# A shorter lead of the max pass, unit 0's maxima in another order, and rows of maxima sent sooner, in an attention and MLP kernel on one core

## The chip, the cores and the metric

The kernel runs on one core of a Trainium2 chip. The metric is the device time of one execution in microseconds, as the median of three runs. Everything told of the inside of an execution comes from one profiled execution.

## The reference

One layer with adaptive layernorm: 2048 tokens of width 512, 32 query heads of width 16 that share one key head and one value head (MQA), then an MLP of width 1376 with a tanh GELU.

```python
mod = (_silu(c) @ w_mod).reshape(c.shape[0], 6, 1, -1)      # sa, ca, ga, sb, cb, gb
h = _layernorm(x) * (1 + ca) + sa
q = (h @ wq) in 32 heads;  k = h @ wk;  v = h @ wv
p = softmax(q @ k.T * Dh ** -0.5);  o = p @ v
x = x + ga * (o @ wo)
h = _layernorm(x) * (1 + cb) + sb
x = x + gb * (gelu(h @ w1 + b1) @ w2 + b2)
```

All of it is float32. The kernel splits the operands of the large products into a high part and the rest (the names that end in H and L) and adds three products.

## The kernel before

**Units.** The 2048 queries are cut into 8 blocks of 256 (`blocks`), and the 32 heads into 8 groups of four. A pair (block, group) is a unit; there are 64, and eight in a row make a block. For a unit, `sexp` forms the scores, one tile e of 128 keys by 512 for each half of the TensorE array, and ScalarE turns it into p with `exp`; `pv` multiplies p with the values into acc. A unit has 8 key steps K, taken in pairs (X, Y), so four pairs, and each pair has two halves.

**Max pass.** Softmax needs each query's maximum first. `Max.step` forms scores once more with queries as rows (tile m, L505), and VectorE reduces each tile to one column of mx (L510). A unit has 32 such products. When its last column is there, `put_max` reduces mx to mm (L558), turns it (`turned`, L559), and `gather` copies four pieces into mt on POOL (L553), splits mt into mh and ml, and `send` writes mh and ml for both halves into two rows of the unit's query tile qst (four transfers, L548). With these rows in qst, the e product subtracts the maximum by itself. So a unit's first e waits for those transfers.

**Lead.** The max pass runs ahead of the units. `lead[u]` is the number of max products done before unit u starts: those of units 0 to u and 4 * LEAD more. Inside a unit each pair issues 8. `first` and `size` count products.

**Clock of steps.** The order on every engine is the order of the program (`manual_schedule`); nothing is reordered. `clock` counts four steps to a pair, 16 to a unit, and `later(n, fn)` issues fn n steps on, through `due()`, in the order of entry. `put_max` enters its reduce so that it falls on the first step of the next pair, the gather MAX_WAIT[0] = 1 step behind it and the sends MAX_WAIT[1] steps behind it. The steps fix only the order in each queue: SP, which issues nearly all transfers, goes ahead until a transfer has to wait.

**Work beside the units.** Jobs in `queue` hand out batches of products, one batch to a pair at most: the late query projections, and for each finished block `rest` (L719): fetch and normalize the attention output (`norm`), the product with wo (wops), layernorm, two transposes (tp) and modulation, w1 with GELU, w2. In `rest_steps`, when the second wops tile is complete (`add_x`, L827), the statistics st follow one and three steps later, `rstd` (mv on VectorE, then ve and rs on POOL) four steps later and `xhat` (xh on POOL) five steps later; the transposes that read xh are offered eight steps later. For every block but the last this happens in the third unit of the next block: wops is complete in the second pair, and the transposes come in the first pair of the fourth unit. In the units behind that each pair carries one w1 tile; its GELU is finished on POOL (L954, L955, L964, L965 and the split into gH and gL).

**Prologue.** Layernorm, keys, values and the first query projections are laid out by hand in SLOTS: each entry says how many max products to issue and then which steps of other work: "q 1" the second query projection, "v 3" values, "rows" the products of the late modulation rows (modl, L290), "wq" casts of wq on ScalarE (wqH, L335). There `later` does its work at once (`draining`). FIRST_MAX says in which order the products of units 0 and 1 come. `keep_warm` issues products whose result is not used (idle, L285); WARM[3] of them stand just ahead of unit 0.

Of the kernel before, what the change touches and what calls it, by code (L numbers as in the profile page):

```python
# [11 lines left out]
ALU = mybir.AluOpType  # L12
AX = mybir.AxisListType

P = 128
# [3 lines left out]

GELU_R = 0.044715 ** 0.5  # L20

LEAD = 6
LEAD_0 = 6
FIRST_MAX = ((0, 0), (1, 0), (0, 1), (1, 1), (0, 2), (0, 3), (1, 2), (1, 3))
SLOTS = ((2, "keys 1", "keys 1"), (2, "keys 1", "keys 1"), (2, "low 1", "heads 2"), (2, "heads 2", "k 1"), (1, "warm"), (1, "heads 2"), (2, "heads 2", "v 0"),
# [4 lines left out]
MAX_WAIT = (1, 4)  # L30
QBUFS = 4
PREP = 4
BUSY = 5
# [3 lines left out]
TAIL = (4, 8)  # L37
GROUP = 4
NORM_WAIT = 6
WARM = (4, 16, 2, 5)  # L40
MOD_WAIT = 3
AHEAD = 4.5
STIR = ((0, 4, 8, 12), (16, 32, 48, 0))
# [2 lines left out]
def raw(ap):  # L46
    return ap.bitcast(F32)
# [3 lines left out]
def adaln_mqa_mlp(  # L51
# [15 lines left out]
    nc = tc.nc  # L67
    _, S, D = x.shape
# [9 lines left out]
    NKC = S // 512  # L78
# [14 lines left out]
    def pad(pool, nbytes, name):  # L93

        nc.gpsimd.memset(pool.tile([P, nbytes // 4], F32, name=name), 0.0)
# [32 lines left out]
    def split(dst_h, dst_l, src, eng_h, eng_l, between=None):  # L128
        if eng_h is nc.gpsimd:
            eng_h.tensor_scalar(out=dst_h, in0=src, scalar1=1.0, scalar2=0.0, op0=ALU.mult, op1=ALU.add)  # L130
        elif eng_h is nc.scalar:
            eng_h.copy(dst_h, src)
        else:
            eng_h.tensor_copy(out=dst_h, in_=src)
        if between:
            between()
        eng_l.tensor_tensor(out=dst_l, in0=src, in1=raw(dst_h), op=ALU.subtract)  # L137
# [7 lines left out]
    def later(n, fn):  # L145
        if draining[0]:
            fn()
        else:
            pending.append((clock[0] + n, fn))
# [7 lines left out]
    def mm3(ps, pairs, every=0, cost=0, begin=True, end=True):  # L157

        n, last = 0, 3 * len(pairs) - 1
        for wh, wl, xh, xl in pairs:  # L160
            for a, b_ in ((wh, xh), (wl, xh), (wh, xl)):
                nc.tensor.matmul(ps, a, b_, start=begin and n == 0, stop=end and n == last)  # L162
                n += 1
                if every and n % every == 0:
                    yield cost
# [113 lines left out]
    def keep_warm(n, **place):  # L279

        for k in range(n):
            if k == 0 or not place:
                ps = psum.tile([P, BQ], F32, name=f"idle{len(idles)}", **(place or dict(tag="m", bufs=3)))
                idles.append(ps)
            nc.tensor.matmul(ps, wkH[:, 0, :], wkH.rearrange("p k n -> p (k n)"), start=True, stop=True)  # L285
# [84 lines left out]
    def turn1(b, d):  # L370
        ps = psum.tile([P, BQ], F32, name=f"tp{b}_{d}", **ebank())
        for t in range(QT):
            nc.tensor.transpose(ps[:, t * P:(t + 1) * P], xts[b][:, t, d * P:(d + 1) * P], ident)
        tps[b, d] = ps
# [40 lines left out]
    def send_q(b, g, qH, qL):  # L415
        for t, src in enumerate((qH, qL)):
            nc.sync.dma_start(out=dq[b][g][t].rearrange("a r j n -> (a r j) n"), in_=raw(src))
        state["q"] -= 1
        sent.add((b, g))
# [3 lines left out]
    def qpairs(b, g):  # L423
        hH, hL = hts[b]
        gs = slice(g * P, (g + 1) * P)
        return [(wqH[:, k, gs], wqL[:, k, gs], hH[:, k, :], hL[:, k, :]) for k in range(KD)]

    def qtiles(b, g):
        qH = att.tile([P, BQ], F32R, name=f"qH{b}_{g}", tag="xH", bufs=2)
        qL = att.tile([P, BQ], F32R, name=f"qL{b}_{g}", tag="xL", bufs=2)  # L430
        return qH, qL

    def qproj(b, g):

        ps = psum.tile([P, BQ], F32, name=f"qps{b}_{g}", tag="v" if g else "x")
        yield from mm3(ps, qpairs(b, g), 3, 1)
        qH, qL = qtiles(b, g)
        if g == 0:
            nc.scalar.copy(qH, ps)
            nc.vector.tensor_tensor(out=qL, in0=ps, in1=raw(qH), op=ALU.subtract)  # L440
        else:
            q32 = pro.tile([P, BQ], F32, name=f"q32_{b}_{g}", tag="h32", bufs=4)
            nc.scalar.copy(q32, ps)
            split(qH, qL, q32, act, pool)
        send_q(b, g, qH, qL)
        yield -2

# [32 lines left out]
    class Max:  # L480


        def __init__(self):
            def products(u, kcs):
                return [(u, j, t, kc) for kc in kcs for j in range(2) for t in range(blocks[units[u][0]][1] // P)]

            def in_rows(u):
                return [(u, j, t, kc) for j in range(2) for t in range(blocks[units[u][0]][1] // P) for kc in range(NKC)]


            begin = [o for u, kc in FIRST_MAX for o in products(u, [kc])]
            self.todo = [begin + [o for u in range(2, NU) for o in in_rows(u)] for _ in range(2)]
            self.mx, self.left, self.done = {}, list(size), 0

# [34 lines left out]
    def put_max(u, mx):  # L529

        T = blocks[units[u][0]][1] // P
        qst = qsts[u]
        mm = mms[u % 2]
        turned = att.tile([P, 32], F32, name=f"turned{u}", tag="turned", bufs=2)
        if u == 0:
            pad(att, 256, "pad7")
        mt = att.tile([4 * T, P], F32, name=f"mt{u}", tag="mt", bufs=2)
        mh = att.tile([4 * T, P], F32R, name=f"mh{u}", tag="mh", bufs=2)  # L540
        ml = att.tile([4 * T, P], F32R, name=f"ml{u}", tag="ml", bufs=2)

        def send():
            for s in range(2):
                for r, src in ((48, mh), (49, ml)):
                    dst = qst[64 * s + r:64 * s + r + 1].rearrange("p j (t n) -> p (j t) n", n=P)
                    ring = nc.scalar if u == 0 and s else nc.sync
                    ring.dma_start(out=raw(dst), in_=raw(src[2 * T * s:2 * T * (s + 1), :].unsqueeze(1)))  # L548
            placed.add(u)

        def gather():
            for g in range(0, P, 32):
                nc.gpsimd.tensor_scalar(out=mt[:, g:g + 32], in0=turned[g:g + 4 * T, :], scalar1=1.0, scalar2=0.0,  # L553
                                        op0=ALU.mult, op1=ALU.add)
            split(mh, ml, mt, nc.gpsimd, nc.gpsimd)

        def reduce():
            nc.vector.tensor_reduce(out=mm[:, :4 * T], in_=mx, axis=AX.X, op=ALU.max)  # L558
            nc.vector.transpose(out=turned, in_=mm)  # L559
            later(MAX_WAIT[0], gather)  # L560
            later(MAX_WAIT[1], send)


        if NQ <= u < NQ + 2:
            reduce()
        else:
            later((0 - clock[0]) % 4 + 1, reduce)
# [613 lines left out]
    act, dve, pool = nc.scalar, nc.vector, nc.gpsimd  # L1181
# [7 lines left out]
    projections = [qproj(b, g) for b in range(2) for g in range(KD)]  # L1189
# [9 lines left out]
    def run(job, n=99):  # L1199
        for _ in range(n):  # L1200
            if next(job, True):
                return
# [23 lines left out]
    def q_group():  # L1226
        for i in range(KD):
            next(projections[0])
            if i == KD - 1:
                next(projections.pop(0))  # L1230
            yield

    def warm():
        keep_warm(WARM[2], tag="x")
        yield
# [17 lines left out]
    turn1(0, 3)  # L1253
    keep_warm(WARM[0])
    mod1(0, 1, pool, dve, lambda: stats1(1))
# [3 lines left out]
    rows = xhat1(1, act)  # L1259
    run(rows, 2)  # L1260

    def first_q(t):
        if t == 1:
            run(q_group())
            load_q(0)
            load_q(1)
# [18 lines left out]
    run(xhat1(3, pool))  # L1285
    keep_warm(WARM[1])
    work = {"keys 1": keys(1), "heads 2": heads(2), "heads 3": heads(3), "q 1": q_group(), "keys 2": keys(2), "keys 3": keys(3),
# [17 lines left out]
    steps = [NKT * blocks[b][1] // BQ for b, _ in units]  # L1305
    lead = [first[u + 1] + 4 * LEAD for u in range(NU)] + [first[NU] + 4 * LEAD]
    for u in range(NQ):
        lead[u] = min(first[1] + 4 * LEAD_0 + (lead[NQ] - first[1] - 4 * LEAD_0) * u / NQ, first[u + QBUFS - 1] - 2)

    def products(batch):  # L1310

        return sum(b_.shape[-1] * (4 if b_.dtype == F32 else 1) for _, _, b_, _, _ in batch) / 512
# [34 lines left out]

    keep_warm(WARM[3], tag="e2", bufs=1)
    behind = None
    for u in range(NU):  # L1350
        for K in range(0, steps[u], 2):
            goal = lead[u] + (lead[u + 1] - lead[u]) * (K + 2) / steps[u]
            goal = min(goal, first[u + QBUFS] if u + QBUFS < NU else first[NU])
            n = max(0, 2 * round((goal - mp.done) / 2))
# [95 lines left out]
    last = queue.pop()[1]  # L1450
# [49 lines left out]
```

## Time and profile before

| | us |
|---|---|
| median of 3 runs (lowest, highest) | 1564.13 (1564.03, 1564.39) |
| span of the profiled execution | 1563.1 |
| PE busy | 1546.5 |
| VectorE (DVE) busy | 1401.7 |
| ScalarE (ACT) busy | 1228.8 |
| GpSimd (POOL) busy | 681.7 |
| first e product of unit 0 | 74.85 |

The span runs from the first to the last instruction of the profiled execution; the device time holds about 1 us more. A row of the timeline has the start, the time, the engine, the line, the operation, the tile written and the tiles read, the shapes and how many instructions were merged; in brackets stands the idle time before it and what ended it. PEld is the weight load of a product; SPq and ACTq are transfers issued by SyncE and ScalarE. In the table by stretches each row has the stretch, its length, and the busy time with the instructions of PE, PEld, DVE, ACT and POOL.

### The profile page before, as it was taken

What the parts mean: (1) busy time and instruction counts of PE and PEld (TensorE: products, weight loads), DVE (VectorE), ACT (ScalarE), POOL (GpSimd) and SP (SyncE); (2) the same over time, 40 slices, a digit from 0 to 9 for tenths busy, and PEclk for the clock granted to TensorE, in tenths of its full rate; (3) what the DMA queues carried; (4) which work ended last, traced back from release to release, by engine and by line L of the source; (5) the groups of instructions that cost most, each with busy time, mean ns of one, the idle gap of its engine ahead of it and who ended that gap; (6) DMA issues with size and microseconds to landing.
All of it is one profiled execution on the core that took longest, in us unless ns stands there. A gap on an engine that the chain in (4) does not pass through costs nothing.

```text
span 1563.1 us, 41433 instructions
## 1 busy us (share of the span) xinstructions
PE 1546.5 (99%) x16387; PEld 959.9 (61%) x16387; DVE 1401.7 (90%) x2479; ACT 1228.8 (79%) x2392; POOL 681.7 (44%) x1194
## 2 busy tenths in 40 slices
PE   7999999999999999999999999999999999999999
PEld 4455555567655665557655675556655676556667
DVE  7999999999999999999999999999999999999625
ACT  5577778788777887788877887788877888788853
POOL 5545433877323570246422472245611573235711
PEclk9999999999999999999999999999999999999999
DMA  7235412313030211213022120303112130312241
GB/s 244 97 96 194 152 52 89 120 52 97 19 110 19 83 60 35 93 29 99 29 62 69 57 84 26 105 16 97 43 50 79 46 97 20 102 34 66 81 150 61
DMA packets 83126, 121.63 MB, mean 78 GB/s; under 512 B 19614, under 2 KB 56222, under 8 KB 82676
## 3 DMA queue, kind: packets, MB, share of 16 engines
q1 hardware_dynamic: 82916, 118.97, 23.5%
q8 instruction: 130, 2.13, 0.6%
q14 instruction: 64, 0.52, 0.1%
q10 hardware_dynamic: 16, 0.00, 0.0%
HBM read 91.13 MB, written 27.27 MB: 76 GB/s over the span
## 4 chain that ended last, share of the span: by engine, by line
PE 84%; DVE 10%; issue 3%; POOL 2%; DMA 1%; ACT 0%; ACTq 0%; SPq 0%; POOLq 0%; DVEq 0%
PE acc L628 28%; PE m L505 24%; PE e L607 16%; DVE mx L510 8%; PE w1ps L191 8%; PE w2ps L181 2%; PE w2ps L191 1%; PE w1ps L181 1%; DMA xt<-in_A_x_dram 1%; PE qps L191 1%; PE tp L191 1%; PE wops L191 1%; PE kps L162 1%; DVE st L835 1%; DVE x L828 1%
## 5 line engine op out<-in xcount | busy, mean ns | idle before, releaser
L510 DVE TENSOR_REDUCE mx<-m 128x1 f32<-128x512 f32 x2048 | 1270.5, 682 | 86.9 <-PE m L505 63.8
L611 ACT ACTIVATE p<-e 128x512 f32<-128x512 f32 x2048 | 1099.3, 598 | 257.4 <-PE e L607 110.5
L505 PE MATMUL m<-ks,qst 64*128 64x512 f32 x2048 | 832.4, 429 | 1.9 <-DVE mx L510 0.6
L607 PE MATMUL e<-qst,ks 64*128 64x512 f32 x2048 | 747.6, 412 | 0.1
L628 PE MATMUL acc<-p,va 128*32 128x256 f32 x8192 | 548.0, 385 | 0.0
L505 PEld LDWEIGHTS m<-ks,qst 64*128 64x128 f32 x2048 | 366.5, 184 | 212.3 <-DVE mx L510 174.8
L607 PEld LDWEIGHTS e<-qst,ks 64*128 64x128 f32 x2048 | 362.5, 184 | 95.2 <-ACT p L611 71.1
L628 PEld LDWEIGHTS acc<-p,va 128*32 128x32 f32 x8192 | 213.7, 109 | 213.1 <-issue 110.0
L553 POOL TENSOR_SCALAR mt<-turned 8x32 f32<-8x32 f32 x256 | 53.1, 208 | 418.9 <-DVE turned L559 406.9
L191 PE MATMUL w1ps<-h2H,w1t 64*128 64x256 f32 x1232 | 235.6, 287 | 0.0
L191 PEld LDWEIGHTS w1ps<-h2H,w1t 64*128 64x128 f32 x1232 | 185.8, 184 | 28.9 <-DVE mx L510 17.7
L191 PE MATMUL w1ps<-h2L,w1t 64*128 64x256 f32 x616 | 169.2, 275 | 0.0
L191 PE MATMUL w2ps<-w2H,gH 64*128 64x512 f32 x284 | 123.8, 436 | 0.0
L191 PEld LDWEIGHTS w1ps<-h2L,w1t 64*128 64x128 f32 x616 | 114.0, 185 | 0.0
L191 PE MATMUL w2ps<-w2L,gH 64*128 64x512 f32 x282 | 110.9, 393 | 0.0
L191 PE MATMUL w2ps<-w2H,gL 64*128 64x512 f32 x282 | 110.2, 391 | 0.0
L954 POOL TENSOR_SCALAR tt<-tt 128x256 f32<-128x256 f32 x77 | 31.0, 403 | 142.6 <-ACT tt L953 109.3
L137 POOL TENSOR_TENSOR gL<-z,gH 128x256 fp32r<-128x256 f32 x77 | 57.0, 740 | 6.4
L955 POOL TENSOR_TENSOR tt<-tt,z 128x256 f32<-128x256 f32 x77 | 56.7, 736 | 6.4
L965 POOL TENSOR_TENSOR z<-tt,z 128x256 f32<-128x256 f32 x77 | 56.4, 733 | 6.0
L964 POOL TENSOR_TENSOR tt<-tt,z 128x256 f32<-128x256 f32 x77 | 56.4, 732 | 0.0
L191 PEld LDWEIGHTS w2ps<-w2H,gL 64*128 64x128 f32 x282 | 52.2, 185 | 0.4
(190 smaller groups left out, 1480.9 us busy)
## 6 DMA issues: line engine op xcount, KB each, us to landing
w1t<-dw SPq DMA_DIRECT2D x82, 512.0 KB
qst<-dq SPq DMA_DIRECT2D x384, 32.0 KB
do<-oc SPq DMA_DIRECT2D x64, 128.0 KB
dw<-w1s SPq DMA_DIRECT2D x11, 512.0 KB
xt<-in_A_x_dram SPq DMA_DIRECT2D x4, 1024.0 KB
dq<-qH SPq DMA_DIRECT2D x16, 256.0 KB
dq<-qL SPq DMA_DIRECT2D x16, 256.0 KB
x<-in_A_x_dram SPq DMA_DIRECT2D x8, 512.0 KB
```

The lines of the kernel that those rows point to most:

```text
L137: eng_l.tensor_tensor(out=dst_l, in0=src, in1=raw(dst_h), op=ALU.subtract)
L181: nc.tensor.matmul(ps, a, b_, start=first_, stop=last_)
L191: ins = nc.tensor.matmul(ps, a[rows], b_[rows], start=first_ and s == 0, stop=last_ and s == 1)
L505: nc.tensor.matmul(m, qsts[u][rows, j, t * P:(t + 1) * P], ks[rows, kc * 512:(kc + 1) * 512], start=True, stop=True)
L510: nc.vector.tensor_reduce(out=self.mx[u][:, i, kc:kc + 1], in_=m, axis=AX.X, op=ALU.max)
L553: nc.gpsimd.tensor_scalar(out=mt[:, g:g + 32], in0=turned[g:g + 4 * T, :], scalar1=1.0, scalar2=0.0, op0=ALU.mult, op1=ALU.add)
L607: nc.tensor.matmul(e, ks[rows, kt * P:(kt + 1) * P], rhs, start=True, stop=True)
L611: ins = nc.scalar.activation(dst, e, AF.Exp, scale=0.25)
L628: ins = nc.tensor.matmul(accs[u][32 * cidx:32 * cidx + 32, :], va[:, kt, :], rhs, start=kt == 0, stop=kt == NKT - 1)
L955: nc.gpsimd.tensor_tensor(out=tt, in0=tt, in1=z, op=ALU.mult)
L964: nc.gpsimd.tensor_tensor(out=tt, in0=tt, in1=z, op=ALU.mult)
L965: nc.gpsimd.tensor_tensor(out=z, in0=tt, in1=z, op=ALU.add)
```

## The change

LEAD and LEAD_0 go from 6 to 4, so the max pass is 16 products ahead instead of 24. FIRST_MAX gets a count in each entry: unit 1's second quarter is cut in two, and unit 0 is complete after 44 products instead of 48. SLOTS issues 48 products instead of 52 (and the loop before unit 0 then fills up to `lead[0]`, 48 instead of 56), starts "q 1" one slot sooner, and `qproj` gets one more step, so that the subtraction on POOL and the transfers of that projection come later than its copies. In `gather`, two of the four copies go to ScalarE for unit 0. MAX_WAIT[1] goes from 4 to 2. The five idle products ahead of unit 0 go (WARM[3] = 0).

```diff
-LEAD = 6
-LEAD_0 = 6
-FIRST_MAX = ((0, 0), (1, 0), (0, 1), (1, 1), (0, 2), (0, 3), (1, 2), (1, 3))
+LEAD = 4
+LEAD_0 = 4
+FIRST_MAX = ((0, 0, 4), (1, 0, 4), (0, 1, 4), (1, 1, 2), (0, 2, 4), (0, 3, 4), (1, 1, 2), (1, 2, 4), (1, 3, 4))
...
-         (0, "v 2"), (2, "q 1"), (2, "q 1"), (2, "q 1"),
-         (2, "q 1", "rows"), (2, "v 3", "wq 2"), (2, "rows"), (2, "rows"), (2, "rows", "wq 3", "load"))
-MAX_WAIT = (1, 4)
+         (0, "v 2", "q 1"), (2, "q 1"), (2, "q 1"), (2, "q 1"), (2, "q 1", "v 3"),
+         (2, "rows", "wq 2"), (2, "rows"), (0, "rows"), (0, "rows", "wq 3", "load"))
+MAX_WAIT = (1, 2)
...
-WARM = (4, 16, 2, 5)
+WARM = (4, 16, 2, 0)
...
-            split(qH, qL, q32, act, pool)
+            nc.scalar.copy(qH, q32)
+            yield -2
+            nc.gpsimd.tensor_tensor(out=qL, in0=q32, in1=raw(qH), op=ALU.subtract)
...
-            begin = [o for u, kc in FIRST_MAX for o in products(u, [kc])]
+            parts = {(u, kc): products(u, [kc]) for u in range(2) for kc in range(NKC)}
+            begin = [parts[u, kc].pop(0) for u, kc, n in FIRST_MAX for _ in range(n)]
...
             for g in range(0, P, 32):
+                if u == 0 and g >= P // 2:
+                    nc.scalar.copy(mt[:, g:g + 32], turned[g:g + 4 * T, :])
+                    continue
...
             if i == KD - 1:
-                next(projections.pop(0))
+                last = projections.pop(0)
+                next(last)
             yield
+        next(last, None)
+        yield
```

More of the change, by code (lines that the diff above doesn't have):

```diff
@@ L488, in in_rows @@
                 return [(u, j, t, kc) for j in range(2) for t in range(blocks[units[u][0]][1] // P) for kc in range(NKC)]
-            begin = [o for u, kc in FIRST_MAX for o in products(u, [kc])]
+            parts = {(u, kc): products(u, [kc]) for u in range(2) for kc in range(NKC)}
+            begin = [parts[u, kc].pop(0) for u, kc, n in FIRST_MAX for _ in range(n)]
+            assert not any(parts.values())
             self.todo = [begin + [o for u in range(2, NU) for o in in_rows(u)] for _ in range(2)]
```

## The prediction, made before the changed kernel was run

> **What bounds the kernel now.** First the page: the span, the two engine rows that matter, and the chain that ended last.
>
> ```profile
> span 1563.1 us, 41433 instructions
> PE 1546.5 (99%) x16387; PEld 959.9 (61%) x16387; DVE 1401.7 (90%) x2479; ACT 1228.8 (79%) x2392; POOL 681.7 (44%) x1194
> PEclk9999999999999999999999999999999999999999
> PE 84%; DVE 10%; issue 3%; POOL 2%; DMA 1%; ACT 0%; ACTq 0%; SPq 0%; POOLq 0%; DVEq 0%
> ```
>
> TensorE is busy nearly always, at nine tenths or more of the full clock in every slice, and makes 84% of the chain; VectorE makes 10%. So time can be won only where PE stands still (the start), and is lost wherever a change makes it stand still. The span is 1563.1 us; the median of the three runs is 1564.13, so about 1.0 us lies around the span, and I add differences to the median. Some 0.2%, 3.1 us, is what a measurement here can tell from no change.
>
> Second, the timeline of the hand-over from the prologue to the units.
>
> ```profile
> 60.38 5.22 DVE L510 TENSOR_REDUCE mx<-m 128x1 f32<-128x512 f32 x8
> 65.10 1.06 PE L290 MATMUL modl<-wml,csb 128*32 128x512 f32 x8
> 66.63 2.48 DVE L510 TENSOR_REDUCE mx<-m 128x1 f32<-128x512 f32 x4 [1.03 <-PE m L505]
> 67.10 0.73 ACT L335 CAST wqH<-wqf 128x256 fp32r<-128x256 f32 x2
> 69.15 0.19 DVE L558 TENSOR_REDUCE mm<-mx 128x8 f32<-128x32 f32 x1
> 69.67 1.02 POOL L553 TENSOR_SCALAR mt<-turned 8x32 f32<-8x32 f32 x4 [0.33 <-DVE turned L559]
> 70.78 0.29 POOL L130 TENSOR_SCALAR mh<-mt 8x128 fp32r<-8x128 f32 x1
> 71.09 1.44 ACTq L548 DMA_DIRECT2D qst<-mh  x1
> 71.15 0.45 POOL L137 TENSOR_TENSOR ml<-mt,mh 8x128 fp32r<-8x128 f32 x1
> 72.63 0.59 ACTq L548 DMA_DIRECT2D qst<-ml  x1
> 73.26 0.73 ACT L335 CAST wqH<-wqf 128x256 fp32r<-128x256 f32 x2 [5.43 <-issue]
> 73.35 1.42 PE L285 MATMUL idle<-wkH 128*128 128x512 f32 x5
> 74.85 0.59 ACT L1302 COPY modl_sb<-modl 128x512 f32<-128x512 f32 x1 [0.86 <-ACT wqH L335]
> 74.85 0.56 PE L607 MATMUL e<-qst,ks 64*128 64x512 f32 x2
> 75.38 4.03 ACT L611 ACTIVATE p<-e 128x512 f32<-128x512 f32 x8
> ```
>
> And the chain of waits in the same place:
>
> ```profile
> 72.63 2.18 DMA qst<-ml
> ```
>
> Unit 0 cannot start before its rows of maxima have landed: the last transfer starts at 72.63, takes 2.18, and the first e follows at 74.85. PE fills the wait with the five idle products at 73.35. Everything back to the last reduce of unit 0 is one chain, so moving that reduce moves the start.
>
> Third, what sets the pace inside a block of eight units. The chain, by line, from 679 to 836 us:
>
> ```profile
> by line: PE acc L628 35.3%; PE m L505 29.8%; PE e L607 19.3%; PE w1ps L191 11.0%; PE w2ps L191 1.9%; PE tp L191 1.1%; PE wops L191 0.9%; DVE mx L510 0.7%; issue 0.1%
> ```
>
> PE alone sets the pace here, with nothing to give back: a PE stall ahead of this stretch is lost for good.
>
> **Part 1: the start.** Before, unit 0 needs 48 products; the four reduces at 66.63 are the last of them, and the eight at 60.38 to 65.60 are numbers 37 to 44. After, unit 0 is complete with number 44, and the projection "q 1" starts one slot sooner, so that its subtraction and its two transfers come behind the rows in the queues of POOL and SP. Reduces 37 to 44 are back to back on DVE, so PE has cover for the earlier projection, and I leave 65.60. So mm starts 69.15 - 65.60 = 3.55 us sooner. Of the four copies at 69.67 (1.02 together) two go to ACT and run beside the others: 0.45 more. Rows land 4.0 us sooner, at 70.8.
>
> What is late next? PE still has the four groups of 1.06 (65.10) and four products. The groups follow the 44th product, at about 65: 4 x 1.06 and the products and transposes (I allow 1.2) end at 70.4, just under 70.8. ACT is nearer: its issues end 4.0 sooner than 73.22, at 69.2, and now both casts (0.73 each, 67.10 and 73.26), a small copy (I allow 0.2) and modl_sb (0.59) follow: 69.2 + 0.73 + 0.73 + 0.2 + 0.59 = 71.45. The first exponential was at 75.38; it comes at 71.45. **The start gains 3.9 us**; if ACT or the groups are later than I think, 2; no more than 4.1.
>
> The five idle products go. Before they filled 1.42 us of a wait; after PE waits some 0.4 us, and the cost is nothing as long as the clock holds, as it does in every slice of the page. The Trainium skill (TensorE: Matmul & The Clock Gate, "What's actually happening") says that about 3.4 us without matmuls halves the clock until a busy window has passed; by it the sum stays, since the gap is shorter, and with a gap over that it would lose some 1.7 us (estimate from that page: half of 3.4).
>
> **Part 2: eight products go to the end.** The lead shrinks from 24 to 16, so eight products (one pair of steps) move from ahead of unit 0 to the second pair of unit 62, where there were none. Busy time by pair, a pair of unit 61 with its maxima and that second pair of unit 62 without:
>
> ```profile
> 1460.94:1466.63 5.69, 5.69 (x74) 4.03 (x75) 5.33 (x10) 4.95 (x12) 3.72 (x6) 1.00 0.24 89
> 1472.22:1477.81 5.59, 5.59 (x68) 3.94 (x64) 1.65 (x6) 4.94 (x11) 4.49 (x10) 1.00 0.02 4
> ```
>
> Both carry a w1 batch. **Cost 0.1 us**, 0.4 at most.
>
> **Part 3: the rows come a pair later in every unit.** With 16 instead of 24, a unit's last maximum falls at the end of the second pair of the unit before it, not the first: 5.69 us later. The sends move from the fourth step behind the reduce to the second: SP runs ahead of the steps and mostly waits for mh, so this matters only where another transfer stands between. In the GELU units there is room (rival 2). The spot where there is none is the third unit of each block, where the layernorm of the previous block runs. There the rows' reduce now falls on step 9, behind the last statistics and before mv and rstd (step 10); the gather falls on step 10 behind rstd, and the normalization xh on step 11. So on DVE mm and turned come before mv, and on POOL the whole gather comes between rs and xh. Unit 26 before:
>
> ```profile
> 665.62 0.49 PE L505 MATMUL m<-ks,qst 64*128 64x512 f32 x1
> 665.71 0.18 DVE L558 TENSOR_REDUCE mm<-mx 128x8 f32<-128x32 f32 x1
> 665.99 0.21 DVE L559 STREAM_TRANSPOSE turned<-mm 128x32 f32<-128x32 f32 x1
> 667.35 0.68 DVE L828 TENSOR_TENSOR x<-wops,x 128x512 f32<-128x512 f32 x1
> 672.20 0.33 DVE L841 BATCH_NORM_AGGREGATE mv<-st 128x2 f32<-128x12 f32 x2
> 672.61 0.24 POOL L842 TENSOR_SCALAR ve<-mv 128x2 f32<-128x2 f32 x1 [4.41 <-DVE mv L841]
> 672.93 0.72 POOL L844 TENSOR_TENSOR rs<-ve,mhalf 128x2 f32<-128x2 f32 x1
> 673.76 4.14 POOL L847 TENSOR_SCALAR xh<-x,mv,rs 128x512 f32<-128x512 f32 x2
> 678.97 0.29 PEld L607 LDWEIGHTS e<-qst,ks 64*128 64x128 f32 x2
> 679.65 0.30 PEld L191 LDWEIGHTS tp<-ident,xh 64*128 64x128 f32 x2
> ```
>
> How often: two xh in each of seven such units.
>
> ```profile
> L847 POOL TENSOR_SCALAR xh<-x,mv,rs x14: 2072/2079/2083, 313.9 to 1396.0; 128x512 f32<-128x512 f32 x14
> ```
>
> The gather takes 71.60 - 69.67 = 1.93 on POOL (its rows at the start). mm and turned take 666.20 - 665.71 = 0.49 on DVE. Before, DVE had to wait there anyway, since the product at 665.62 ends at 666.11: taking them away wins nothing, and x at 667.35 follows the products of the same half pair. From there DVE has no pause up to mv at 672.20, so two more operations ahead of mv make it 0.4 to 0.5 later. The second xh ends at 677.90 before, and the transposes load it from 679.65: 1.75 us of slack. The change uses 0.49 + 1.93 = 2.42, so PE waits 0.67; consecutive operations overlap by a few hundredths, so 0.6. If mv does not move, 1.93 - 1.75 = 0.2.
>
> The rows of unit 27 are bounded the same way: mh ends at rs's end 673.65 + 0.49 + 0.1 + 1.40 = 675.64 (1.40 from 69.67 to 71.07), the fourth transfer starts 2.07 later (712.46 to 714.53 below), and with the 2.18 of the start they land at 679.89, when e was due at 678.97: 0.9 late at most, and mostly beside the same stall. That 2.18 was ACT's; SP's own landing has no row. The Trainium skill (DMA: Bandwidth & Descriptors, "Anatomy of one DMA") gives a fixed cost of about 2.0 us, measured on another path; by it the bound would be 0.7. I take the xh value, 0.6 for each of seven blocks: **4.2 us**, bounds 1.4 (0.2 each) and 6.3 (0.9 each).
>
> **Sum**: -3.9 + 0.1 + 4.2 = +0.4, so 1564.13 + 0.4 = **1564.5 us**: no change that can be told. This case by itself reaches from 1561.7 (0.2 each) to 1567.0 (0.9 each).
>
> **Rival 1, the third unit costs nothing**: DVE catches up before mv, or PE makes good the wait behind the transposes. For it: DVE has pauses in most other half pairs. Against: PE alone makes the chain behind it. Then -3.9 + 0.1 = -3.8: 1560.3.
>
> **Rival 2, slower: rows land late in the GELU units.** Rows for unit 29, sent in unit 28:
>
> ```profile
> 709.69 0.21 DVE L559 STREAM_TRANSPOSE turned<-mm 128x32 f32<-128x32 f32 x1
> 712.46 0.68 SPq L548 DMA_DIRECT2D qst<-mh  x1
> 714.12 0.74 POOL L964 TENSOR_TENSOR tt<-tt,z 128x256 f32<-128x256 f32 x1
> 714.53 0.57 SPq L548 DMA_DIRECT2D qst<-ml  x1
> 723.69 0.19 PEld L607 LDWEIGHTS e<-qst,ks 64*128 64x128 f32 x1
> ```
>
> They land by 714.53 + 2.18 = 716.71; 5.69 later is 722.40, 1.3 us ahead of e at 723.69. If the gather falls behind one more GELU tail, four POOL operations of up to 0.74 (2.9 us), they are 1.6 late. It decides once POOL lags 1.3 us more than now. For it: POOL is strictly in order. Against: the gather moves by a whole pair, and the GELU repeats every pair, so the order stays. In one unit of each block: 7 x 1.6 = 11 us, 1564.5 + 11 = 1575.7.
>
> **Rival 3, the start does not move as far**: ACT or the groups hold the first exponential and half is won, 2 us. Then -2.0 + 0.1 + 4.2 = +2.3: 1566.4, still no change that can be told.
>
> **Chances.** Forecast 0.62, rival 1 0.18, rival 2 0.08, rival 3 0.12. Below 1561.0 lies nearly all of rival 1: faster 0.17. Above 1567.3 lie rival 2, a little of rival 3 and the upper edge of the forecast: slower 0.13. Same 0.70. The range for 8 in 10 takes in most of rival 1 and rival 3 and leaves rival 2 out: 1560.2 to 1567.3.
>
> **What would show it.** Right: the first e at about 70.9 and the first exponential at about 71.5; no idle products; in the seven third units POOL runs ve, rs, mt, mh, ml, xh in that order, and the tp loads follow xh at once, 0.6 later against the unit's start than before; the second pair of unit 62 at 5.7. Wrong: xh ahead of the gather, or tp not waiting (rival 1); e in other units released by the rows' transfer (rival 2); the first exponential behind 73 (rival 3).

## The result, and the profile after

The changed kernel takes 1578.91 us (median of 5 runs, 1574.25 to 1579.87) beside 1564.14 for the kernel before (5 runs, 1564.03 to 1565.55): ratio 1.0083, 95% interval 1.0072 to 1.0094. It is about 14.8 us slower, where no change was forecast. The rows of the page that answer to those of before:

```profile
span 1577.1 us, 41417 instructions
PE 1552.3 (98%) x16382; PEld 963.8 (61%) x16382; DVE 1401.3 (89%) x2479; ACT 1229.8 (78%) x2394; POOL 680.8 (43%) x1192
PEclk9899999999999999999999999999999999999999
L614 PE MATMUL e<-qst,ks 64*128 64x512 f32 x2048 | 750.8, 413 | 6.0 <-DMA qst<-ml 6.0
```

The work is the same; the span grew by 14.0 us. One slice of the clock is no longer full, and e now waits 6.0 us in all for the rows of maxima, at the starts of units 0, 10 and 12. Where the 14.0 us lie is read from the first e (its weight load) of units 0, 1, 9, 13 and 63 in the two traces (us; the differences are mine):

| stretch | before | after | more |
|---|---|---|---|
| start to unit 1's first e | 96.93 | 101.32 | 4.39 |
| units 1 to 8 | 178.35 | 178.49 | 0.14 |
| units 9 to 12 | 88.50 | 96.05 | 7.55 |
| units 13 to 62 | 1124.57 | 1126.62 | 2.05 |
| unit 63 and the end | 74.80 | 74.59 | -0.21 |

**The start.** Unit 0's first e came at 79.14, not at the forecast 70.9. The timeline after (idle time and its releaser in brackets):

```profile
55.14 0.68 DVE L400 TENSOR_TENSOR ks<-kps,ks 16x512 fp32r<-16x512 f32 x1
55.85 0.62 ACT L404 CAST ks<-ks 16x512 fp32r<-16x512 f32 x1 [0.75 <-DVE ks L400]
55.87 1.15 PE L509 MATMUL m<-ks,qst 64*128 64x512 f32 x2 [0.89 <-DVE ks L400]
56.52 0.18 PEld L509 LDWEIGHTS m<-ks,qst 64*128 64x128 f32 x1 [0.47 <-ACT ks L404]
65.96 0.80 PE L162 MATMUL qps<-h0H,wqH 128*128 128x512 f32 x1
68.37 1.29 DVE L514 TENSOR_REDUCE mx<-m 128x1 f32<-128x512 f32 x2 [1.61 <-PE m L509]
74.00 0.19 DVE L565 TENSOR_REDUCE mm<-mx 128x8 f32<-128x32 f32 x1
75.09 0.29 POOL L130 TENSOR_SCALAR mh<-mt 8x128 fp32r<-8x128 f32 x1
79.14 0.34 PEld L614 LDWEIGHTS e<-qst,ks 64*128 64x128 f32 x2 [1.79 <-issue]
```

The new FIRST_MAX puts unit 0's third key quarter at product 29, where unit 1's second quarter stood. That product needs key block 2, whose low part (L400) and its repeat (L404) are only being made: m waits at 55.87 and again at 56.52. Product 37 waits for key block 3 in the same way (0.87 us, at 64.62). Behind that a product of the query projection takes 0.80 us (65.96) that took 0.51 before, and VectorE, whose reduces were back to back before, waits for products. The table by stretches shows both; first two rows of before, then four of after, columns as in the prediction (the seventh number is the granted clock):

```profile
60.00:70.00 10.00, 9.72 (x51) 3.72 (x49) 8.71 (x16) 2.87 (x7) 3.03 (x6) 1.00 0.14 54
70.00:80.00 10.00, 9.48 (x59) 4.20 (x57) 8.91 (x16) 5.29 (x11) 2.96 (x8) 1.00 0.09 21
```

```profile
56.00:58.00 2.00, 1.85 (x7) 0.87 (x7) 1.34 (x2) 1.42 (x4) 0.77 (x2) 1.00 0.00 0
60.00:62.00 2.00, 2.00 (x7) 0.85 (x5) 1.29 (x2) 0.00 (x0) 0.00 (x0) 0.52 0.00 0
60.00:70.00 10.00, 8.98 (x26) 4.37 (x24) 5.93 (x9) 2.56 (x5) 0.00 (x0) 0.67 0.01 2
70.00:80.00 10.00, 9.09 (x52) 3.70 (x54) 5.42 (x11) 3.98 (x11) 4.09 (x8) 0.89 0.14 53
```

Between 60 and 70 us VectorE made 9 operations where it had made 16, at a clock of 0.67.

**Units 9 to 12.** The timeline of POOL, SP and PE at the end of unit 11, after:

```profile
339.64 1.28 POOL L1139 TENSOR_TENSOR w2f<-w2f,gb 128x512 f32<-128x512 f32 x1
342.96 1.30 POOL L1139 TENSOR_TENSOR w2f<-w2f,gb 128x512 f32<-128x512 f32 x1
345.04 1.29 POOL L137 TENSOR_TENSOR w2L<-w2f,w2H 128x512 fp32r<-128x512 f32 x1
346.31 1.02 POOL L560 TENSOR_SCALAR mt<-turned 8x32 f32<-8x32 f32 x4
349.78 0.57 SPq L552 DMA_DIRECT2D qst<-ml  x1
351.55 0.46 PE L614 MATMUL e<-qst,ks 64*128 64x512 f32 x1 [4.19 <-DMA qst<-ml]
```

Two steps of the w2 preparation (339.64 to 346.3, `prep_w2`) stand ahead of the gather of unit 12's rows in POOL's queue, so the rows land when PE has been waiting for 4.19 us. Unit 11 took 26.47 us, 21.94 before. The same happens on a smaller scale at the end of unit 9: a w2 step ends at 296.6, the gather of unit 10's rows follows it, and PE waits 0.93 us for them (303.07). Unit 9 took 23.22 us, 21.98 before.

**The third units.** Unit 26 after:

```profile
684.66 0.17 DVE L565 TENSOR_REDUCE mm<-mx 128x8 f32<-128x32 f32 x1
684.93 0.21 DVE L566 STREAM_TRANSPOSE turned<-mm 128x32 f32<-128x32 f32 x1
685.72 0.72 POOL L851 TENSOR_TENSOR rs<-ve,mhalf 128x2 f32<-128x2 f32 x1
686.52 1.01 POOL L560 TENSOR_SCALAR mt<-turned 8x32 f32<-8x32 f32 x4
687.11 0.18 PEld L509 LDWEIGHTS m<-ks,qst 64*128 64x128 f32 x1 [0.41 <-DVE mx L514]
687.99 0.45 POOL L137 TENSOR_TENSOR ml<-mt,mh 8x128 fp32r<-8x128 f32 x1
688.44 4.14 POOL L854 TENSOR_SCALAR xh<-x,mv,rs 128x512 f32<-128x512 f32 x2
692.63 0.18 PEld L191 LDWEIGHTS tp<-ident,xh 64*128 64x128 f32 x1
```

The order on POOL is the forecast one, rs, gather, xh, and the transposes of the second xh load at its end (692.58). But that costs PE nothing: unit 27, in which they stand, takes 21.92 us in both kernels. What grew is unit 26: 22.10 us, 21.78 before, so 0.32 and not 0.6. It grew ahead of xh's end, in one half of a pair: 3.01 us from 686.13 on, where before took 2.68. There m waits at 687.11 for a reduce of VectorE, and the reduces start 0.49 us behind the last statistics where before had 0.15, since mm and turned stand between. Before, the same load did not wait:

```profile
674.33 0.18 PEld L505 LDWEIGHTS m<-ks,qst 64*128 64x128 f32 x1
```

### The profile page after: what moved, and what is told of

It reads as the page before. It is cut to its first block, busy times and chain, and to the rows that moved or that the text cites. A ratio compares the mean times of both kernels' runs of the same rounds, so it can differ in the third digit from the quotient of the medians.

```text
span 1577.1 us, 41417 instructions
## 1 busy us (share of the span) xinstructions
PE 1552.3 (98%) x16382; PEld 963.8 (61%) x16382; DVE 1401.3 (89%) x2479; ACT 1229.8 (78%) x2394; POOL 680.8 (43%) x1192
## 4 chain that ended last, share of the span: by engine, by line
PE 91%; DVE 5%; DMA 1%; POOL 1%; ACT 1%; issue 0%; SPq 0%; DVEq 0%; POOLq 0%
PE acc L635 31%; PE m L509 26%; PE e L614 17%; PE w1ps L191 8%; DVE mx L514 4%; PE w2ps L191 2%; PE w2ps L181 2%; PE wops L191 1%; PE qps L191 1%; PE w1ps L181 1%; DMA xt<-in_A_x_dram 1%; PE tp L191 1%; PE kps L162 1%; DMA qst<-ml 0%; PE wops L181 0%; PE tp L373 0%
```

## The experiments

What has to be told apart: theory 1 says that the order costs the start (key block not ready, VectorE stands still, clock falls) and that the shorter lead costs units 9 to 12 (POOL's w2 steps ahead of the gather) and the third units. Against it stand the removed idle products as the cause of the fallen clock, and GELU or layernorm work as the cause in units 9 to 12. The ratio is that of the medians of all executions, with the kernel before run beside each; the other columns (us) are read from one profiled execution of each kernel. "9 to 12" and "13 to 62" are the lengths of those units. Unit 63 and the end, not in the table, took 74.5 to 76.0 us, in no relation to the edits.

| kernel | ratio to before (95%) | first e | unit 1 starts | 9 to 12 | 13 to 62 |
|---|---|---|---|---|---|
| before | | 74.85 | 96.93 | 88.50 | 1124.57 |
| after | 1.0083 (1.0072, 1.0094) | 79.14 | 101.32 | 96.05 | 1126.62 |
| a_lead6 | 1.0060 (1.0037, 1.0083) | 78.02 | 100.96 | 88.93 | 1124.32 |
| a_order | 1.0065 (1.0050, 1.0080) | 73.51 | 97.47 | 95.23 | 1126.27 |
| a_both | 1.0010 (1.0001, 1.0019) | 73.51 | 97.33 | 88.47 | 1124.23 |
| a_atonce | 1.0138 (1.0118, 1.0158) | 75.87 | 98.04 | 90.33 | 1140.91 |
| b_warm | 1.0011 (1.0002, 1.0020) | 75.74 | 97.82 | 88.49 | 1124.23 |
| b_hold | 1.0043 (1.0030, 1.0057) | 73.18 | 96.56 | 94.17 | 1126.23 |
| b_k2 | 1.0025 (1.0014, 1.0035) | 76.60 | 101.06 | 88.56 | 1124.21 |
| b_wait4 | 1.0061 (1.0045, 1.0076) | 74.15 | 96.44 | 96.01 | 1126.42 |
| c_fix | 1.0018 (1.0009, 1.0027) | 74.36 | 98.28 | 90.11 | 1126.70 |
| c_lead0 | 1.0024 (1.0015, 1.0032) | 73.41 | 95.47 | 89.07 | 1124.48 |
| c_best | 1.0017 (1.0007, 1.0026) | 72.68 | 94.76 | 88.68 | 1124.30 |
| d_gap | 1.0012 (1.0003, 1.0021) | 75.84 | 98.26 | 88.65 | 1124.35 |

**a_lead6: the changed kernel with the lead of before.**

```diff
-LEAD = 4
-LEAD_0 = 4
+LEAD = 6
+LEAD_0 = 6
```

> The changed kernel with LEAD and LEAD_0 back at 6. Theory 1 (the lag of the rows behind POOL's weight steps in units 9 to 12 and behind rstd in the third units costs some 9.5 us, the start 4.3): the units take their old lengths again, the start stays late, 1568 to 1571 us. Rival (all of it comes from the lower granted clock of this kernel): the units stay long, 1576 to 1580.

1574.44 us, above the expected 1568 to 1571; the four executions took 1570.78 to 1578.68, and the profiled one is the fastest of them. Units 9 to 12 and the third units are back at the times of before, the start is not: first e at 78.02. So the lead costs the steady part, and something else the start.

**a_order: the changed kernel with the order of before.**

```diff
-FIRST_MAX = (..., (1, 1, 2), (0, 2, 4), (0, 3, 4), (1, 1, 2), (1, 2, 4), (1, 3, 4))
+FIRST_MAX = (..., (1, 1, 4), (0, 2, 4), (0, 3, 4), (1, 2, 4), (1, 3, 4))
```

> The changed kernel with unit 1's second quarter whole again in FIRST_MAX, so unit 0 is complete with product 48. Theory 1 (product 29 stands ahead of the copies of the third key block, PE waits 2 us for them and the granted clock falls behind that wait): the clock holds at 60 to 72 us, first e at 72.5 to 75 instead of 79.1, 1572 to 1575 us. Rival (the idle products that were taken out had held the clock): the clock falls all the same, first e at 77 or later, 1577 to 1580.

1575.1 us, a tenth above theory 1's range; the first e, at 73.51, lies inside it, and the clock holds from 60 to 72 us as theory 1 says. Units 9 to 12 keep their loss. But the clock falls later. In the table by stretches PE has nothing to do while it waits for the rows, and runs at half speed when they have come:

```profile
68.00:72.00 4.00, 1.70 (x16) 0.26 (x8) 0.71 (x3) 0.50 (x3) 1.19 (x5) 1.00 0.02 7
72.00:76.00 4.00, 2.48 (x11) 1.65 (x12) 1.72 (x3) 3.08 (x7) 1.64 (x3) 0.80 0.17 45
76.00:80.00 4.00, 4.00 (x25) 1.94 (x25) 3.15 (x6) 2.20 (x5) 0.00 (x0) 0.50 0.02 5
```

Unit 0 takes 23.96 us, 22.08 before. The rival had the time of the first e wrong, but a part of it stands: the clock falls without the idle products all the same, if behind the first e.

**a_both: both edits.** What is left of the change are the gather on two engines, the earlier "q 1", the rows two steps sooner, and no idle products.

> Both of these: lead 6 and the old order; left of the change are the earlier second projection, the copies on ScalarE, the sends two steps sooner and no idle products. Theory 1: all losses gone, 1562.5 to 1565. Rival (the idle products or the sooner sends cost by themselves): 1567 or more.

1566.99 us, 1.0010 (1.0001 to 1.0019), above the expected 1562.5 to 1565 and at the edge of the rival's 1567; before took 1565.30 beside it. From unit 1 to unit 62 it runs as before does. Its first e comes 1.34 us sooner and unit 0 takes 1.74 longer (23.82): the products at half speed, 0.99 for a pair of e that took 0.56.

```profile
73.57 0.99 PE L614 MATMUL e<-qst,ks 64*128 64x512 f32 x2
```

These three kernels give the split. The lead: a_order less a_both, 6.8 us in units 9 to 12 and 2.0 behind them. The order: a_lead6 less a_both, 4.5 us at the first e. In these two the first e does not wait for the rows alone: in a_lead6 the last transfer of the rows starts at 72.74, and eight leading products, paced by VectorE, still stand ahead of the first e at 78.02. So the 4.5 us are what VectorE lost by the order. The reduce mm itself comes at 70.05 in a_lead6 and at 68.38 in a_both.

**a_atonce: the maxima of every unit reduced in the pair that completes them**, so that the gather enters POOL's queue ahead of that pair's w2 steps.

```diff
-        if NQ <= u < NQ + 2:
+        if u:
```

> The changed kernel with the rows' reduce of every unit but the first done at once (step 6 instead of 9), so the gather stands on step 7, ahead of the weight step of step 8 and of rstd on step 10. Theory 1 (the place of the gather in POOL's queue is what costs): units 9 to 12 and the third units take nearly their old lengths, the start stays late, 1568 to 1571 us. Rival (the smaller lead itself starves something else, the place does not matter): 1577 to 1580.

1586.33 us, a miss. Units 9 to 12 did what was expected (90.33), but nearly all the other units grew by some 0.3 us each: 16.3 us more than before from unit 13 on, 15.0 of it in the third pairs. The timeline of unit 14, in its third pair:

```profile
400.68 1.28 DVE L514 TENSOR_REDUCE mx<-m 128x1 f32<-128x512 f32 x2
401.99 0.18 DVE L565 TENSOR_REDUCE mm<-mx 128x8 f32<-128x32 f32 x1
402.21 0.21 DVE L566 STREAM_TRANSPOSE turned<-mm 128x32 f32<-128x32 f32 x1
402.35 2.44 DVE L514 TENSOR_REDUCE mx<-m 128x1 f32<-128x512 f32 x4
403.05 0.18 PEld L509 LDWEIGHTS m<-ks,qst 64*128 64x128 f32 x1 [0.28 <-DVE mx L514]
```

mm and turned now stand inside a run of reduces, and the next product's load waits behind them for a free m. That this pause is the whole 0.3 was read from the trace, not tried. It is the pause that the third units have in the changed kernel.

**b_warm: a_both with the five idle products back.** `WARM = (4, 16, 2, 5)`.

> The kernel with 24 leading products and the first unit's key quarters in the order of before, now with the five idle products back ahead of the first e. Theory 1 (the start's gain was eaten by the clock: without the idle products the granted clock was 0.66 over 70 to 80 us and unit 0 took 23.82 us where before took 22.08): the clock stays at 0.95 or more over 70 to 80 us, the first e comes at 73.5 to 74.0, unit 0 takes 22.0 to 22.4, and the kernel ends 0.8 to 1.6 us ahead of before (1562.5 to 1563.5 where before takes 1564.1; ratio 0.9990 to 0.9995). Rival (the idle products stand in TensorE's queue ahead of the first e, five of about 0.4 us, and cost what they save): first e at 75 or later, ratio 1.000 to 1.001.

1.0011. The clock stays at 1.00 and unit 0 takes 22.08, as theory 1 has it, but the first e comes at 75.74, as the rival has it: the five now follow the last leading product, with no wait left to fill. Their row and that of the first e:

```profile
74.38 1.43 PE L285 MATMUL idle<-wkH 128*128 128x512 f32 x5
75.74 0.50 PE L614 MATMUL e<-qst,ks 64*128 64x512 f32 x2
```

1.43 us for the products, 1.74 for the clock without them: the 1.34 won at the gather goes either way. Most of the rest of the lateness is a start that ran 0.6 later (the copy of the last key block, L404, at 61.06 instead of 60.46). The five may not hold the clock every time: in 4 of the 11 executions its mean over the whole kernel is 0.998 or less, as it is in all ten of a_both; where it fell in those is not shown.

**b_hold: a_order without w2 steps at the end of a second pair.**

```diff
-... weights[0] in preps and not state["busy"]:
+... weights[0] in preps and not state["busy"] and not (weights[0] == "w2" and K == 2):
```

> The kernel with 16 leading products and the order of before, in which GpSimd's steps that prepare w2 are not started at the end of a unit's second pair, the place that lies ahead of the gather in GpSimd's queue. Theory 1 (units 9 to 12 grow because one or two w2 steps of 3.3 us stand ahead of the gather, and the rows then land after the next unit wants them): from the first e of unit 9 to that of unit 13 the kernel takes 88.5 to 90.5 us, where the same kernel without the hold took 95.2 and before 88.5; it ends 4.5 to 6.5 us ahead of that kernel (1572.8 in the profiled execution), at 1567 to 1569. Rival (the loss there is ScalarE's and GpSimd's work for the second layer norm, which waits for the shorter lead whatever w2 does): 94 us or more, time as without the hold (1573 to 1576).

Unit 11's stall is gone (21.94 us, 26.47 in a_order), but units 9 to 12 still take 94.17: the w2 steps moved into unit 12, among the GELU's steps on POOL. ScalarE waits for POOL, the exponentials behind it wait, and e waits for them:

```profile
351.94 0.42 ACT L965 ACTIVATE tt<-tt 128x256 f32<-128x256 f32 x1 [2.24 <-POOL tt L962]
352.89 0.18 PEld L614 LDWEIGHTS e<-qst,ks 64*128 64x128 f32 x1 [1.90 <-ACT p L618]
355.16 0.75 POOL L971 TENSOR_TENSOR tt<-tt,z 128x256 f32<-128x256 f32 x1
```

The kernel takes 1572.37 us, above theory 1's 1567 to 1569. The place was named rightly and little time was won; units 9 to 12 fit the rival's number, though not its reason.

**b_k2: a_lead6 with four idle products behind each of the two key steps.**

```diff
-         (2, "low 2", "k 2", "v 1", "wq 1"), ... (2, "low 3", "k 3"),
+         (2, "low 2", "k 2", "idle", "v 1", "wq 1"), ... (2, "low 3", "k 3", "idle"),
+    def idle():
+        while True:
+            keep_warm(4)
+            yield
```

> The kernel with 24 leading products and the changed kernel's order (unit 0's third key quarter pulled ahead of half of unit 1's second), with four idle products put ahead of each of the two products that wait for key blocks 2 and 3, to hold the clock over the waits. It splits what the new order costs at the start (first e 78.02 with the new order, 73.51 with the old one). Theory 1 (the waits themselves cost about 1.3 us each, since VectorE's reduces, which set the pace of the start, stand still; the fallen clock costs the rest, about 2 us): clock 0.97 or more up to 70 us, first e at 75.3 to 76.8. Rival (all of it is the wait, the clock hides behind VectorE): first e at 77.5 to 79 with the clock held. Third reading (all of it is the clock): first e at 73.5 to 74.5.

The clock stays at 1.00 up to 70 us and the first e comes at 76.60, in theory 1's range. So of the order's 4.5 us some 3.1 are the waits (76.60 - 73.51, with the idle products' own time in it) and 1.4 the clock, in one execution each. The reduce mm comes at 68.62, no sooner than the 68.38 of a_both, though unit 0 needs four products less: the waits eat all that the order was to win. Unit 1 starts no sooner than in a_lead6, since here the clock fell later (0.88 and 0.78 over 70 to 90 us).

**b_wait4: a_order with the sends four steps behind.** `MAX_WAIT = (1, 4)`.

> The kernel with 16 leading products and the order of before, with the rows sent four steps after the maxima are gathered up (as before) rather than two. Theory 1 (in most units ml ends 17.8 us into the unit and the sends follow it at once, so that the send's place in the queue does not decide; four steps later puts it about 18.5 us in, and the rows end at 20.6 where they ended at 19.9, landing still ahead of the next unit at 22.8): time within 3 us of the same kernel with two steps (1573 to 1578). Rival (the later sends land after the next unit's first e wants them): 0.5 to 1.5 us in each of some fifty units, 1600 to 1640.

1574.79 us beside 1575.1 for a_order: no difference that can be told, as theory 1 expected. The rows "two steps sooner" do nothing here. Up to unit 0 this kernel does the same as a_order, with the same wait ahead of the first e (3.84 and 3.82 us), yet unit 0 takes 22.29 us where a_order took 23.96: the clock over 72 to 84 us was 0.86 here and 0.72 there. So what a fallen clock costs unit 0 differs from one execution to the next.

**c_fix: a_order, and the maxima of units 8 to 12 reduced at once.** The w2 steps stay where they are.

```diff
-        if NQ <= u < NQ + 2:
+        if NQ <= u < NQ + 5:
```

> The kernel with 16 leading products and the order of before, in which the maxima of units 8 to 12 (not 8 and 9 alone) are reduced in the pair in which they are complete, so that the gather of units 10 to 12 enters GpSimd's queue ahead of the w2 steps that are started at that pair's end, and the w2 steps themselves stay where they are. Theory 1 (the w2 steps ahead of the gather, and nothing else, make units 9 to 12 longer; holding them back only moved the cost to unit 12's GELU): from the first e of unit 9 to that of unit 13 the kernel takes 89.3 to 90.6 us, where it took 95.2 without the edit and before took 88.5; all else as without the edit, so 1568.5 to 1571. Rival (the queue of GpSimd is too full there with the shorter lead, wherever the gather stands): 93 us or more, 1572 to 1576.

Units 9 to 12 take 90.11 and the kernel 1568.5 us, both at or inside theory 1's ranges. The gather of unit 12's rows stands ahead of the w2 steps now:

```profile
336.63 1.02 POOL L560 TENSOR_SCALAR mt<-turned 8x32 f32<-8x32 f32 x4
338.52 1.27 POOL L1139 TENSOR_TENSOR w2f<-w2f,gb 128x512 f32<-128x512 f32 x1
```

5.1 of a_order's 6.7 us over before are back; this shows the queue as the cause.

**c_lead0: a_both, the first units with the lead of 16, later ones with 24, eight idle products.** `LEAD_0 = 4`, `WARM = (4, 16, 2, 8)`.

> The kernel with the order of before in which only the first units lead by 16 products and the later ones by 24, with eight idle products ahead of the first e. The first e then stands behind 48 products in TensorE's queue, not 56, so the idle products run while TensorE waits for the rows (about 69.5 to 73.2 us) and cost nothing. Theory 1: first e at 73.0 to 73.8, clock 0.97 or more over 70 to 80 us, unit 0 takes 22.1 to 22.4, ratio to before 0.9985 to 0.9998. Rival (first units with the shorter lead take longer, or the clock falls all the same): unit 0 at 23 or more, ratio 1.000 to 1.002.

**c_best: the same, with two of unit 1's products behind unit 0's last, not four.** `FIRST_MAX = (..., (1, 1, 3), (0, 2, 4), (0, 3, 4), (1, 1, 1), ...)`.

> As the kernel with 16 leading products for the first units alone and eight idle products, with two of unit 1's products of the second key quarter (not four) put behind unit 0's last: unit 0's maxima are complete at product 46, not 48, and no product that wants key block 2 comes before the third pair of products after that block's chain. Theory 1 (a product may be pulled ahead only as far as its key block is there): the reduce of unit 0's maxima starts 1.3 us sooner, no new wait for key block 2, first e at 71.7 to 72.7, ratio to before 0.9975 to 0.9992. Rival (the next product still meets the wait for the keys, and VectorE stands still): first e at 73.5 or later, ratio 0.9995 to 1.001.

The start did what theory 1 says in both: first e at 73.41 and 72.68, clock 1.00, unit 0 at 22.06 and 22.08, so unit 1 starts 1.5 and 2.2 us ahead of before. An order that asks for a key block no sooner than it is there is worth 0.7 us of the 1.3 expected; c_best's start ran 0.75 later in this execution (L404 at 61.01, 60.26 in c_lead0), so that the order may be worth twice that. Yet both kernels are slower than before. Units 1 to 8 take 183.6 us in both where before takes 178.35: there the eight products that were not made ahead of unit 0 are made up, two each in the first pairs of units 1, 3, 5 and 7. The table by stretches of c_best, the first pair of unit 1, which has 10 products, and the third, which has 8:

```profile
94.76:101.36 6.60, 6.60 (x64) 3.74 (x65) 6.03 (x11) 4.80 (x10) 2.72 (x4) 1.00 0.41 105
107.42:113.12 5.70, 5.70 (x62) 3.35 (x63) 5.13 (x10) 4.27 (x8) 1.90 (x7) 1.00 0.01 2
```

5.2 us for eight products is 0.65 each: some 1 us in each of those first pairs, and the rest in the pairs behind them. A shorter lead ahead of unit 0 is a debt, not a gain.

**d_gap: a_both with one idle product behind each of the leading products but the last.**

```diff
     while mp.done < lead[0]:
         chunk(1)
+        if mp.done < lead[0]:
+            keep_warm(1, tag="e2", bufs=1)
```

> The kernel with 24 leading products and the order of before, without the block of idle products but with one idle product behind each of the last leading products but one (seven in all), where TensorE waits 0.4 us for VectorE each time. Theory 1 (the idle products cost 1.4 us only where they stand in a row behind the last product; the clock needs products, not their place): first e at 73.3 to 74.0, clock 0.97 or more over 70 to 80 us, unit 0 takes 22.0 to 22.4, so unit 1 starts 0.8 to 1.5 us ahead of before's 96.93; ratio to before 0.9990 to 1.0002. Rival (seven idle products in the gaps are too few for the clock, or push the products apart): clock under 0.9 and unit 0 at 23 or more, or first e at 74.8 or later; ratio 1.000 to 1.002.

1.0012; the rival was right in its second half. The clock stays at 1.00 (unit 0: 22.42), but the leading products come every 0.86 us where a_both has them every 0.60:

```profile
70.72 0.18 PEld L509 LDWEIGHTS m<-ks,qst 64*128 64x128 f32 x1 [0.25 <-issue]
71.15 0.19 PEld L285 LDWEIGHTS idle<-wkH 128*128 128x128 f32 x1 [0.24 <-issue]
71.57 0.18 PEld L509 LDWEIGHTS m<-ks,qst 64*128 64x128 f32 x1 [0.24 <-issue]
```

At each change between the two kinds of product the weight load stands still for 0.24 us. First e: 75.84. No version tried beats the kernel before.

## Why the prediction was wrong, step by step

**Part 1, the step that failed first:** "Reduces 37 to 44 are back to back on DVE, so PE has cover for the earlier projection, and I leave 65.60." mm came at 74.00, 8.4 us later. I had counted how many products stand ahead of unit 0's last and not asked which key block each one reads. Numbers 29 and 37, the first to read blocks 2 and 3, now come before these are there. a_order, which keeps the projection and has mm at 68.34, shows that this order, and not the projection, makes the start late; by b_k2 about two thirds of it are the waits. That share is not settled: in a_atonce, which has the same prologue as the changed kernel, mm came at 70.73 and not at 74.00, with the clock at half for a shorter time.

**Part 1, the gather** did what was said: mm to mh took 1.63 us before and 1.09 after. a_both shows its worth at the first e together with the earlier "q 1": 1.34.

**Part 1, the idle products:** "the cost is nothing as long as the clock holds". It did not hold. In a_both the clock fell and unit 0 paid 1.74 us. That the sentence beside it, which named the Trainium skill, had put the price at 1.7 is luck: four kernels with one and the same wait ahead of unit 0 (a_order, c_fix, b_hold and b_wait4) paid 1.9, 1.8, 1.3 and 0.2. What failed is the condition: the sum took the clock of before for granted in a kernel that removes what had helped to hold it.

**Part 2** was right: unit 62 takes 21.81 us, 21.71 before (the 0.1 lies in its first pair; the second takes 5.58). c_lead0 and c_best show that it hangs on the place: the eight products cost 0.1 where the pair had none, and 5.2 on top of the eight in each pair of units 1 to 8.

**Part 3** came near with the wrong wait. The order on DVE and POOL came as forecast, but the step "The change uses 0.49 + 1.93 = 2.42, so PE waits 0.67" failed: PE does not wait behind xh, and unit 27 is not longer. So far rival 1 was right. The 0.3 of each third unit comes from a path that was not in the sum: mm and turned delay not only mv but the reduces behind it, and PE waits for a free m. This is read from the traces (the same half of a pair grows by 0.19 to 0.33 us in all seven third units) and was not tried alone. a_order less a_both gives 2.0 us from unit 13 on, six such units and the 0.1 of unit 62. In the sum itself the upper bound is 1566.6 (-3.9 + 0.1 + 6.3), not 1567.0; nothing hangs on it. That the place of the sends "matters only where another transfer stands between" is borne out by b_wait4.

**What was not in the sum at all:** 7.55 us in units 9 to 12. Rival 2 had the mechanism, "the gather falls behind" other POOL work and the rows land late, but looked for it in the GELU, which repeats every pair. The work that had no second chance was the one-time w2 preparation, which I had not looked at, as I read a block in the middle and took it for all. c_fix shows the cause. Of the 7.55, unit 11 has 4.5, unit 9 1.2 and unit 10 0.2. About 1.5 us come behind the stall, in unit 12 (24.35 us, 22.80 before), at a fallen clock:

```profile
352.00:354.00 2.00, 2.00 (x17) 1.80 (x13) 1.37 (x2) 1.20 (x2) 0.00 (x0) 0.51 0.15 44
```

So a forecast of -3.9 + 0.1 + 4.2 stands beside +4.4, +0.1, +2.0 and +7.6.

## What to carry to other kernels

When an order is changed, check for each moved item when its inputs are ready, not only how many items stand ahead of it. When slack is shortened everywhere, look for the one stretch where a queue is fullest (a preparation that runs once), not for the stretch that repeats most. Work with an unused result may be holding a clock: before it is taken out, find what else keeps the array busy there, and if it is put back, see that it lies in a wait.

## What the runs showed of the hardware

The clock fell without a long pause. In the changed kernel no wait of PE between 54 and 58 us is longer than 0.9 us (PE was busy for 1.11 of the 2 us from 54 on and for 1.85 of the next 2), yet over 60 to 62 us the clock is 0.52. The Trainium skill (TensorE: Matmul & The Clock Gate, "What's actually happening") ties the fall to an idle window of about 3.4 us; this trace shows it falling for products that come thinly, so the measurement decides: a gap under 3.4 us is no safety. Nor does it fall every time: a_lead6 has the same wait of 0.89 us at 54.83, and its clock stays at 1.00 up to 64 us. In a_order, where PE stood still from 69.7 to 73.5 (3.8 us), the rule and the trace agree.

The scatter goes with that fall: the five executions of the changed kernel lie at 1574.25 and 1575.71 with a mean clock of 0.998, and at 1578.91 to 1579.87 with 0.991 to 0.996. a_lead6 shows the same, 1570.78 and 1571.81 with 0.997 and 0.995, 1577.07 and 1578.68 with 0.991 and 0.992. a_atonce, whose prologue is the same, had a clock of 0.83 where after had 0.67 (60 to 70 us), and its first e 3.3 us sooner.
